# Column sums of the exponentials on TensorE: two tiles each for groups 2 to 7

## The chip, the cores and the metric

The kernel runs on one core of a Trainium2 chip. Five engines work at once, each on its own queue in order: TensorE (PE in the profile, its weight loads PEld), VectorE (DVE), ScalarE (ACT), GpSimd (POOL) and SyncE (SP, which here only starts transfers). The metric is the device time of one execution in microseconds; lower is better.

## The reference

The input is `q`, `k`, `v` for 8 batches, 12 heads, 448 tokens and 64 channels. Cut to what matters:

```
q_n, k_n = rmsnorm(q, g_q), rmsnorm(k, g_k)
scores = q_n @ k_n^T / 8
attn = exp(scores) / sum(exp(scores))       # per query, over the keys
x = attn @ v, heads side by side            # (8, 448, 768)
s = x @ w_gate                              # per token
top 128 tokens of each batch by s:
    out = x + sigmoid(s) * (relu(x @ w1) @ w2)
all other tokens: out = x
```

The change is in the `sum(exp(scores))`, the denominator of the attention, which is a sum over keys for every query.

## The kernel before

All arithmetic is in float32. The work is cut into 24 groups of four heads (three groups a batch, `NG` = 3), and each group into seven units (`NI` = 7) of 64 keys, 168 units in all. Unit `u` is unit `u % 7` of group `u // 7`.

For a unit, `scores` (L290) lets TensorE multiply keys and queries into two score banks out of four (`ps_sc`), and ScalarE takes the exponential of each bank (L299) into a tile `p` of 128 x 2 x 448 numbers. `p` has seven buffers. `values` (L316) multiplies `p` with the values and sums all seven units of a group in two banks `av`; `values_out` copies these away on ScalarE (L343).

Keys lie on the partitions of `p`, so the denominator is a sum over partitions and over the seven tiles of a group. The tiles are first added together on VectorE: `add_probs` (L333) starts with the sum of tiles 0 and 1 in a tile `sum` (two buffers) and adds one more tile at each further unit, a 128 x 896 addition each. `sum_keys` (L362) then sums over the partitions on TensorE: four matmuls with a constant 128 x 32 matrix `pick_pair` write four strips of 32 rows of a bank `den_ps`, 224 columns each. ScalarE copies the bank to `den` (L370), `invert_sums` transposes it on TensorE (L377) and VectorE takes the reciprocals (L379). `to_tokens` transposes the attention output on TensorE (L391), and VectorE multiplies it with the reciprocals into `x` (L393).

For some groups the last tile is not added on VectorE. `add_probs` keeps it in `lasts`, and `sum_keys` puts it through four more matmuls into the same bank, as a second term beside `sum`. Before the change this holds for groups 0 to 5 and for the last one: `sums_last` is `n < 2 * NG or n == n_groups - 1`.

The order of all engines is written out by hand. A loop over `q` issues four units a turn: the scores of two units, the values of the two before them, twice over. Between the pairs stand the pieces of the gated feed-forward part of an earlier batch (`mixture`, L525 to L572) and the `tasks`: `finish` queues, for each group that has ended, `sum_keys`, `invert_sums` and two `to_tokens`. `den_ps`, `denT_ps` and `x_ps` share one bank (`ps_aux`), or one of another pool where no mixture runs, so each of them waits until the one before it has been read.

The other work that the prediction steps on:

- `squares` (L202, ScalarE) and `sum_squares` (L208 on VectorE, L209 and L212 on GpSimd) make the norms of a later group from its tile `tok`; `rows_out` (L226, GpSimd's queue) and `rows_in` (L238, SP's queue) spread them over partitions as `bc`, and `scale_q` (L247, VectorE) scales the queries.
- At the end of a batch `gate` and `spread` (L417 to L438, VectorE) make the gate scores, `score_rows` (L446 on TensorE, L450 on ScalarE) turns them into rows, `count` (L460, VectorE) ranks the tokens with four compare instructions, `annotate` (L475 to L479, VectorE) writes the ranks, and `select` (L487, four indirect transfers on GpSimd's queue) gathers the best 128 tokens in a buffer in memory. `load_selected` (L505) reads them back through SP's queue. That queue works in order and also carries all input tiles (L61), the feed-forward weights (L190) and `bc`.

Of the kernel before, what the change touches and what calls it, by code (L numbers as in the profile page):

```python
# [68 lines left out]
def fast(  # L69
# [27 lines left out]
    NI = S // D  # L97
    H = 2 * NP
    GH = 4
    NG = H // GH  # L100
# [7 lines left out]
    n_groups = B * NG  # L108
# [18 lines left out]
    def aux(shape, name):  # L127

        if PER * now[0] >= units:
            return ps_sc.tile(shape, F32, tag="sc", name=name)  # L130
        if spare[0]:
            return ps_moe.tile(shape, F32, tag="moe", name=name)
        return ps_aux.tile(shape, F32, tag="aux", name=name)
# [144 lines left out]
    probs, sums, avs, xTs, rdens, xs = {}, {}, {}, {}, {}, {}  # L278
# [44 lines left out]

    def add_probs(u):
        n, i = divmod(u, NI)
        if i == NI - 1 and sums_last(n):
            lasts[n] = probs.pop(u)
            probs.pop(u - 1)
            return
        if i > 0:  # L330
            if i == 1:
                sums[n] = p_pool.tile([128, 2, S], F32, name="sum", bufs=2)
            nc.vector.tensor_tensor(  # L333
                out=sums[n], in0=probs[u - 1] if i == 1 else sums[n], in1=probs[u], op=OP.add
            )
            probs.pop(u - 1)
        if i == NI - 1:
            probs.pop(u)

    def values_out(n):  # L340
# [5 lines left out]

    dens, lasts = {}, {}

    def sums_last(n):


        return n < 2 * NG or n == n_groups - 1

    def sum_keys(n):

        ps = aux([128, 512], "den_ps")
        terms = [sums.pop(n)] + ([lasts.pop(n)] if n in lasts else [])
        for t in terms:
            for hh in range(2):
                for odd in range(2):  # L360
                    o = 64 * odd + 32 * hh
                    nc.tensor.matmul(  # L362
                        out=ps[o : o + 32, 0 : S // 2],
                        lhsT=pick_pair,
                        rhs=t[:, hh].rearrange("k (jj odd p) -> k odd jj p", odd=2, p=CP)[:, odd],
                        start=(t is terms[0]),
                        stop=(t is terms[-1]),
                    )
        den = norm_pool.tile([128, NJ // 2, CP], F32, name="den", bufs=1)
        nc.scalar.copy(out=den.rearrange("d j p -> d (j p)"), in_=ps[:, 0 : S // 2])  # L370
        dens[n] = den
# [268 lines left out]
    def finish(n, q):  # L640

        if n == n_groups - 1:
            for fn, args in ((sum_keys, (n,)), (invert_sums, (n,)), (to_tokens, (n, 0))):
                task((q, 1), fn, *args)
            task((q, 1), last_tokens, n)
            return
        task((q, 1), sum_keys, n)
        task((q, 2), invert_sums, n)
        task((q + 1, 0), to_tokens, n, 0)
        task((q + 1, 1), last_tokens, n)  # L650
# [35 lines left out]
    def run_values(upto, q):  # L686
        ended = False
        while waiting and waiting[0] <= upto:
            u = waiting[0]
            if ended and u % NI == 0:  # L690

                return
            values(waiting.pop(0))
            if u % NI == NI - 1:
                values_out(u // NI)
                finish(u // NI, q)
                ended = True
            add_probs(u)
# [580 lines left out]
```

## Time and profile before

| what | value |
|---|---|
| median of 4 runs | 534.6 us (534.34 to 536.62) |
| the profiled execution, its own time | 534.5 us |
| its span, first to last instruction | 532.8 us |
| what lies around the span | 1.7 us |
| mean granted TensorE clock | 0.993 of full speed |

An execution that is profiled gives for every instruction its engine, its line in the code, its start and its duration. A group of equal instructions is written with its count ("x8"), a TensorE group by pipelined matmuls whose durations overlap, so that the distance from one group's start to the next one's, not the duration, is what a group costs. A float32 matmul of the code shows as two records: four matmuls on a `p` tile are "x8". "[0.47 <-ACT den L370]" says that the engine sat idle for 0.47 us before the group and which instruction let it go on.

Busy share of three engines, the clock and the transfers in the stretch where groups 2 to 7 end, from the table of windows (the share of the 16 DMA engines can come out a little over 1):

| stretch, us | length | PE busy | DVE busy | ACT busy | DMA share |
|---|---|---|---|---|---|
| 52 to 64 | 12 | 10.58 | 10.46 | 9.55 | 0.69 |
| 64 to 78 | 14 | 13.35 | 13.55 | 10.89 | 0.63 |
| 78 to 86 | 8 | 7.74 | 7.38 | 5.49 | 1.02 |
| 86 to 94 | 8 | 7.53 | 7.54 | 6.64 | 1.05 |
| 94 to 103 | 9 | 8.65 | 6.91 | 6.08 | 0.81 |
| 103 to 111 | 8 | 7.44 | 5.98 | 6.09 | 1.03 |
| 111 to 126 | 15 | 14.32 | 14.20 | 10.92 | 1.01 |
| 126 to 140 | 14 | 14.00 | 11.95 | 8.29 | 1.06 |
| 140 to 150 | 10 | 10.00 | 5.47 | 4.75 | 0.88 |

The column sums of groups 2 to 7 start on TensorE at 59.00, 76.39, 92.47, 101.86, 118.20 and 142.45 us.

### The profile page before, as it was taken

How to read it: one execution, taken by the hardware profiler on the slowest of the kernel's cores; microseconds unless marked ns; L12 is line 12 of the kernel's file. 1: busy time of each engine (PE TensorE's matmuls, PEld its weight loads, DVE VectorE, ACT ScalarE, POOL GpSimd, SP SyncE). 2: the span in 40 equal slices, each digit the busy share in tenths (PEclk: the TensorE clock that was granted, in tenths of full speed). 3: DMA queues.
4: the chain of work that ended last, by engine and by line, in shares of the span. 5: the costliest groups of instructions: out<-in, count | busy, mean ns of one | idle time of the engine just before them, and what ended most of it. 6: DMA issues, size and time to landing. Idle time of an engine off the chain costs nothing. (4 is left out here: it accounts for less than half of the span.)

```text
span 532.8 us, 16470 instructions
## 1 busy us (share of the span) xinstructions
PE 505.9 (95%) x7116; PEld 285.2 (54%) x7116; DVE 339.7 (64%) x644; ACT 277.9 (52%) x506; POOL 240.6 (45%) x193
## 2 busy tenths in 40 slices
PE   6999899899999999999999999999999999999991
PEld 5444344346644466546644466543665457568770
DVE  2777899789675776659657795668766385443000
ACT  3687787684635755546545755547554354311000
POOL 4784997756724276244734456336742103002000
PEclk9999999999999999999999999999999999999997
DMA  8957859899971497608736486604945032004100
GB/s 300 357 167 250 269 197 345 293 348 292 337 218 36 131 266 219 207 31 222 247 113 209 124 265 208 222 4 126 294 126 139 32 106 62 1 30 134 61 4 33
DMA packets 41605, 93.57 MB, mean 176 GB/s; under 512 B 6454, under 2 KB 24374, under 8 KB 41524
## 3 DMA queue, kind: packets, MB, share of 16 engines
q1 hardware_dynamic: 36772, 85.96, 50.9%
q0 software_dynamic: 4608, 6.47, 3.7%
q8 instruction: 58, 0.95, 0.7%
q14 instruction: 23, 0.19, 0.1%
q10 hardware_dynamic: 144, 0.00, 0.0%
HBM read 74.93 MB, written 25.35 MB: 188 GB/s over the span
## 5 line engine op out<-in xcount | busy, mean ns | idle before, releaser
L299 ACT ACTIVATE p<-sc,rinv 128x448 f32<-128x448 f32 x336 | 186.3, 641 | 101.7 <-PE sc L290 89.4
L290 PE MATMUL sc<-qT,kT 64*32 64x448 f32 x2688 | 151.6, 540 | 0.9 <-ACT p L299 0.6
L316 PE MATMUL av<-p,v 64*32 64x448 f32 x2688 | 146.6, 537 | 0.0
L212 POOL TENSOR_TENSOR rinv<-ss,neg_half 128x14 f32<-128x14 f32 x48 | 137.8, 2872 | 4.0
L333 DVE TENSOR_TENSOR sum<-sum,p 128x896 f32<-128x896 f32 x113 | 122.5, 1084 | 8.9 <-ACT p L299 1.8
L316 PEld LDWEIGHTS av<-p,v 64*32 64x32 f32 x2688 | 54.9, 107 | 71.9 <-issue 65.6
L209 POOL TENSOR_SCALAR ss<-ss 128x14 f32<-128x14 f32 x48 | 22.1, 461 | 155.1 <-DVE ss L208 129.0
L290 PEld LDWEIGHTS sc<-qT,kT 64*32 64x32 f32 x2688 | 48.8, 106 | 71.4 <-issue 47.9
L544 PE MATMUL moe_ps<-xeT,w 128*128 128x128 f32 x576 | 69.2, 277 | 0.0
L544 PEld LDWEIGHTS moe_ps<-xeT,w 128*128 128x128 f32 x576 | 66.2, 192 | 4.3 <-issue 4.3
L393 DVE TENSOR_TENSOR x<-x_ps,rden 112x512 f32<-112x512 f32 x48 | 32.9, 689 | 51.3 <-PE x_ps L391 51.1
L208 DVE TENSOR_REDUCE ss<-sq 128x14 f32<-128x896 f32 x48 | 51.3, 1076 | 22.4 <-ACT sq L202 19.3
L563 PE MATMUL moe_ps<-w,hT 128*128 128x384 f32 x176 | 61.2, 491 | 0.0
L487 POOL DMA_INDIRECT selected<-x,rank x32 | 36.1, 1127 | 35.0 <-DVE x L479 26.2
L202 ACT ACTIVATE sq<-tok 128x896 f32<-128x896 f32 x48 | 46.0, 964 | 8.9 <-DMA tok<-in_tok_dram 8.6
L581 POOL DMA_INDIRECT out_dram<-xe,row x8 | 10.8, 1346 | 77.6 <-DVE rden L379 45.6
L563 PEld LDWEIGHTS moe_ps<-w,hT 128*128 128x128 f32 x176 | 31.7, 190 | 21.8 <-issue 2.9
L417 DVE SCALAR_TENSOR_TENSOR prod<-x,wg 112x256 f32<-112x256 f32 x96 | 40.9, 426 | 3.0
L226 POOL DMA_DIRECT2D rows<-rinv x44 | 29.1, 662 | 6.5 <-POOL rinv L212 6.5
L391 PEld LDWEIGHTS x_ps<-ident,xT 128*112 128x112 f32 x192 | 21.0, 134 | 18.9 <-issue 11.9
L391 PE MATMUL x_ps<-ident,xT 128*112 128x128 f32 x192 | 29.1, 278 | 1.4 <-DVE x L393 1.4
L572 DVE SCALAR_TENSOR_TENSOR xe<-sc,xe 128x384 f32<-128x384 f32 x5 | 3.1, 618 | 41.0 <-PE sc L563 41.0
(66 smaller groups left out, 341.2 us busy)
## 6 DMA issues: line engine op xcount, KB each, us to landing
tok<-in_tok_dram SPq DMA_DIRECT2D x48, 448.0 KB, 6.7
qT<-in_qT_dram SPq DMA_DIRECT2D x24, 448.0 KB, 4.9
kT<-in_kT_dram SPq DMA_DIRECT2D x24, 448.0 KB, 9.1
v<-in_vp_dram SPq DMA_DIRECT2D x24, 448.0 KB, 7.2
out_dram<-x SPq DMA_DIRECT2D x8, 1344.0 KB
bc<-rows SPq DMA_DIRECT2D x44, 224.0 KB, 5.7
xe<-selected SPq DMA_DIRECT2D x8, 385.0 KB, 3.0
w<-in_moe_w_dram SPq DMA_DIRECT2D x6, 512.0 KB
```

What stands on the lines that cost most here:

```text
L202: nc.scalar.activation(out=sq, in_=t, func=AF.Square, scale=scale)
L208: nc.vector.tensor_reduce(out=ss, in_=sq, axis=AX.X, op=OP.add)
L212: nc.gpsimd.tensor_tensor(out=rinv.rearrange(flat), in0=ss.rearrange(flat), in1=neg_half.to_broadcast([128, 2 * NI]), op=OP.pow,)
L290: nc.tensor.matmul(out=scs[hh][o : o + 32, 0:S], lhsT=get("kT", n)[r, c, D * i + k0 : D * i + k0 + 32], rhs=get("qT", n)[r, c, :], start=True,
L299: nc.scalar.activation(out=p[:, hh], in_=scs[hh][:, 0:S], func=AF.Exp, scale=rinvs[n, 1][:, hh, i : i + 1],)
L316: nc.tensor.matmul(out=avs[n][c][o : o + 32, 0:S], lhsT=get("v", n)[r, hh, i, d0 : d0 + 32], rhs=probs[u][r, hh], start=(i == 0), stop=(i ...
L333: nc.vector.tensor_tensor(out=sums[n], in0=probs[u - 1] if i == 1 else sums[n], in1=probs[u], op=OP.add)
L391: nc.tensor.transpose(out=ps[:CP, j, :], in_=t[:, j, :], identity=ident)
L417: nc.vector.scalar_tensor_tensor(out=prod, in0=xs[b][:, j, cols], scalar=1.0, in1=wg[:, cols], op0=OP.mult, op1=OP.mult, accum_out=gates[b ...
L487: w = nc.gpsimd.indirect_dma_start(out=t[:, :], out_offset=bass.IndirectOffsetOnAxis(ap=rank[:, j : j + 1], axis=0), in_=x[:, j, :], in_of ...
L544: nc.tensor.matmul(out=ps[:, 128 * i : 128 * i + n], lhsT=w1[:, dc, 128 * (f0 + i) : 128 * (f0 + i + 1)], rhs=xeT[:, dc, :n], start=(dc == 0),
L563: nc.tensor.matmul(out=ps[:n, : DM // 2], lhsT=hT[:, fc, :n], rhs=w2[:, fc, cols], start=(fc == 0), stop=(fc == NFC - 1),)
```

## The change

`sums_last`, a yes or no for each group, becomes `held`, a count: one tile for groups 0, 1 and 23, two for groups 2 to 7, none for the others. `add_probs` no longer adds a held tile on VectorE, and `sum_keys` puts each held tile through its own four matmuls. `lasts[n]` is a list. Tiles 0 and 1 are let go together at unit 1 and each later one at its own unit, which is bookkeeping in the program that builds the kernel.

```diff
     def add_probs(u):
         n, i = divmod(u, NI)
-        if i == NI - 1 and sums_last(n):
-            lasts[n] = probs.pop(u)
-            probs.pop(u - 1)
+        if i >= NI - held(n):
+            lasts.setdefault(n, []).append(probs.pop(u))
             return
         if i > 0:
             if i == 1:
                 sums[n] = p_pool.tile([128, 2, S], F32, name="sum", bufs=2)
             nc.vector.tensor_tensor(
                 out=sums[n], in0=probs[u - 1] if i == 1 else sums[n], in1=probs[u], op=OP.add
             )
-            probs.pop(u - 1)
-        if i == NI - 1:
+            if i == 1:
+                probs.pop(u - 1)
             probs.pop(u)
...
-    def sums_last(n):
-        return n < 2 * NG or n == n_groups - 1
+    def held(n):
+        return 1 if n < 2 or n == n_groups - 1 else 2 if n < 8 else 0
...
-        terms = [sums.pop(n)] + ([lasts.pop(n)] if n in lasts else [])
+        terms = [sums.pop(n)] + lasts.pop(n, [])
```

Instruction by instruction this leaves ScalarE's, GpSimd's and SP's queues as they were. TensorE gets four more matmuls in the column sums of groups 2, 3, 4 and 5 and eight more in those of groups 6 and 7, 32 in all, each time right behind the matmuls that are there. VectorE loses one addition for each of groups 2 to 5 and two for each of groups 6 and 7, eight in all. Nothing else changes its place.

## The prediction

> **What bounds the kernel now.** I read the page first, then the table of windows around the changed groups, then the timelines of TensorE, ScalarE, VectorE and SP there, then the landings of the transfers.
>
> ```profile
> span 532.8 us, 16470 instructions
> PE 505.9 (95%) x7116; PEld 285.2 (54%) x7116; DVE 339.7 (64%) x644; ACT 277.9 (52%) x506; POOL 240.6 (45%) x193
> ...
> L333 DVE TENSOR_TENSOR sum<-sum,p 128x896 f32<-128x896 f32 x113 | 122.5, 1084 | 8.9 <-ACT p L299 1.8
> ```
>
> TensorE is busy for 95% of the span. The change takes 8 additions of 1.084 us (8.7 us) off an engine with 64% and gives 32 matmuls to the full one. So each added matmul counts unless TensorE would have stood idle, and an addition saved counts only where TensorE, in the end, waits for VectorE. I go through the six places.
>
> **What one held tile costs on TensorE.** With one held tile (group 5) the column sums take from 101.86 to the next group of instructions at 102.76, 0.90 us; with none (group 7) from 142.45 to 142.97, 0.52 us. The difference, 0.38 us, is the price of four matmuls of this form; the distance from the first term's start to the second's (92.47 to 92.87) gives 0.40. Eight such tiles are 8 x 0.38 = 3.0 us if none is hidden. Four matmuls are eight records of 0.35 us, so they overlap: they run in four column strips.
>
> [...]
>
> **Groups 2 and 3: hidden behind ScalarE.**
>
> ```profile
> 61.39 0.43 PE L377 MATMUL denT_ps<-ident,den 128*112 128x128 f32 x2 [1.42 <-DVE prod L417]
> ...
> 78.27 0.43 PE L377 MATMUL denT_ps<-ident,den 128*112 128x128 f32 x2 [0.91 <-ACT den L370]
> ```
>
> ```profile
> 60.95 0.38 ACT L370 COPY den<-den_ps 128x224 f32<-128x224 f32 x1
> ...
> 77.88 0.34 ACT L370 COPY den<-den_ps 128x224 f32<-128x224 f32 x1
> ```
>
> TensorE stands still before the transposition of the sums, because ScalarE has to copy them first. In group 2 the matmuls end at 59.97, but ScalarE reaches the copy at 60.95, behind a square of another group, with no idle time; its end at 61.33 is what releases TensorE (the releaser that the line names, one of VectorE's products, is only the nearest event). With 0.40 more the sums end at 60.37: no cost. In group 3 they end at 77.35, the copy starts at 77.88, again behind a square; group 4 shows that ScalarE starts 0.07 after the last matmul. 77.35 + 0.40 + 0.07 = 77.82: just in time, no cost. Without that cover each would cost 0.38.
>
> **Groups 4 and 5: paid, then swallowed.**
>
> ```profile
> 92.87 0.56 PE L362 MATMUL den_ps<-p,pick_pair 128*32 128x224 f32 x8
> 93.90 0.43 PE L377 MATMUL denT_ps<-ident,den 128*112 128x128 f32 x2 [0.47 <-ACT den L370]
> ...
> 102.27 0.56 PE L362 MATMUL den_ps<-p,pick_pair 128*32 128x224 f32 x8
> 102.76 1.73 PE L290 MATMUL sc<-qT,kT 64*32 64x448 f32 x32
> 104.28 1.71 PE L316 MATMUL av<-p,v 64*32 64x448 f32 x32
> 106.56 2.18 PE L290 MATMUL sc<-qT,kT 64*32 64x448 f32 x25 [0.56 <-ACT p L299]
> ...
> 110.55 0.43 PE L377 MATMUL denT_ps<-ident,den 128*112 128x128 f32 x2
> ```
>
> ```profile
> 104.78 0.95 ACT L202 ACTIVATE sq<-tok 128x896 f32<-128x896 f32 x1 [3.18 <-DMA tok<-in_tok_dram]
> 105.64 0.33 ACT L370 COPY den<-den_ps 128x224 f32<-128x224 f32 x1
> 105.87 4.55 ACT L299 ACTIVATE p<-sc,rinv 128x448 f32<-128x448 f32 x8
> ```
>
> In group 4 ScalarE waits for the sums (its copy starts at 93.50 after 0.35 idle), so TensorE falls back by 0.40; in group 5 by another 0.38, 0.78 at 102.76. But here TensorE is ahead of ScalarE. Two scores and two values take 1.52 + 1.51 + 1.51 + 1.64 = 6.18 us where nothing waits (elsewhere in this timeline), and 102.76 to 110.55 is 7.79: 1.61 lost. ScalarE stands 3.18 us before a square whose tile lands at 104.7, and the exponentials queue behind it without a gap until 110.4; the scores of the next pair need their banks. That landing belongs to SP's queue: the tile is issued at 99.00 behind `xe` (97.17), which waits for the last of the four gathers (landed 97.15), which GpSimd issues after work that starts at 81.51 with a sum of squares of VectorE. None of it hangs on TensorE after 81. Being 0.78 late fits in 1.61, so the stretch ends with ScalarE and this 0.78 costs nothing. The other end: if the landing moves with TensorE, 0.78 is paid in full.
>
> **The saving on VectorE.** VectorE works almost without a gap from 64.98 to 86.63 (20.58 busy of 21.65). Only one removed addition, group 3's at 74.28, lies ahead of a chain that someone waits for: the queries' scaling (its `bc` landed by 74.96, so it can start a microsecond earlier), then the four compares from 77.35, then the sum of squares above. The compares need ScalarE's rows, which end at 77.03, so this moves up by 0.27 at most, and through gathers, SP and tile to ScalarE at 104.78. The stretch is full of transfers (DMA share 1.02 to 1.05 from 78 to 94), where an earlier issue need not land as much earlier. Bounds 0 and -0.27; I take the middle, -0.15. The other seven additions end in front of waits that are not VectorE's own lateness: before the output scaling at 59.11, 101.12 and 117.46 it idles for TensorE already (1.16, 1.36, 0.33), group 4's scaling at 86.63 has nothing waiting behind it before 92.47, and at 136.92 it waits for ScalarE.
>
> **Groups 6 and 7: two tiles each, paid.**
>
> ```profile
> 118.20 0.58 PE L362 MATMUL den_ps<-sum,pick_pair 128*32 128x224 f32 x8 [0.46 <-DVE x L393]
> 119.01 0.55 PE L525 MATMUL moe_ps<-ident,xe 128*128 128x128 f32 x3 [0.22 <-ACT xeT L530]
> 119.39 0.38 PE L377 MATMUL denT_ps<-ident,den 128*112 128x128 f32 x2
> ```
>
> ```profile
> 142.45 0.58 PE L362 MATMUL den_ps<-sum,pick_pair 128*32 128x224 f32 x8
> 142.97 2.94 PE L544 MATMUL moe_ps<-xeT,w 128*128 128x128 f32 x24
> ```
>
> Group 6: the 0.46 before the sums is the bank's turn (VectorE reads the output of the instruction before) and stays. Behind them stands a wait of 0.22 that the new matmuls fill. Then the transposition needs the copy: in group 4 it starts 93.90 - 92.47 = 1.43 after the sums' start with one held tile, with two 1.43 + 0.40 = 1.83, so at 120.03 in place of 119.39: +0.64. Bounds: +0.54 (0.76 less 0.22, if the copy is quicker) and +0.76. Group 7: nothing waits on TensorE from 126 to 150, and 2.8 us of feed-forward matmuls hide the copy: 2 x 0.38 = +0.76, with bounds 0.76 and 0.80.
>
> A held tile also keeps its buffer until the column sums. `p` has seven; tiles 5 and 6 of a group are wanted again by the scores seven units later, and at the sums at most three units beyond the group are scored, so nothing waits for them. Behind 150 the few waits of TensorE (0.29 to 1.22 us) are its own round trips over ScalarE and VectorE and move with it, as does the tail.
>
> **The sum.** 0 + 0 + 0.78 - 0.78 - 0.15 + 0.64 + 0.76 = +1.25 on the profiled execution's 534.5 us (span 532.8 and 1.7 around it), 535.75; the median is 0.1 above that execution, so 535.8.
>
> **Rivals.**
>
> Slower: the wait for the tile at 104.78 swallows nothing. If transfers that TensorE frees late (queries, keys and values wait for its reads in SP's queue) push the tile back by as much as TensorE is late, the 0.78 stays: 0.78 + 0.64 + 0.76 = +2.2, 536.8. It decides once the landing is more than 0.5 later. For it: the DMA engines are full there. Against it: everything in the queue ahead of the tile is issued before 99.00, and only group 4's delay (0.40) precedes that. If group 3's cover, 0.06 wide, fails as well, 537.2; all eight paid is 537.6.
>
> Faster: the relief of VectorE is worth more, because gathers and tile land out of the crowd of weights that are issued from 86.64 on. TensorE can win back no more than the 1.61, of which 0.78 is spent: -0.83. With groups 6 and 7 paid that is +0.57, 535.2; to fall under 534.6 their 1.40 must be hidden too, at the lowest 533.8. For it: VectorE has no gap from 65 to 87. Against it: the compares wait for ScalarE's rows, and 126 to 150 has no idle time to hide in.
>
> Without effect, the additions having been the same work: excluded by the counts, 64 more records on a full engine.
>
> **How the numbers follow.** The forecast has 0.55, with its own range 535.1 (chain full early, bounds low) to 536.4; the slower rival 0.33, the faster one 0.12. What this kernel's measurement can tell from no change is about 0.3%, 1.6 us. The forecast lies within it but for 0.06 that comes out above 536.2; all of the slower rival lies above; of the faster one 0.08 is put beyond the bound for something that the trace doesn't show, 0.04 within. Faster 0.08, same 0.53, slower 0.39. The range 534.7 to 537.1 leaves out the faster rival's low part and the slower one's upper end.
>
> **What would show it.** Records of the sums over held tiles 120 in place of 56, additions 105 in place of 113, VectorE's busy time near 331 us. Groups 2 and 3: transposition still at 61.4 and 78.3. Group 4: 94.3. Then the wait of TensorE near 106.6 shrunk and 110.55 reached at 110.3 to 110.6; a start near 111.3 there would be the slower rival. Group 6's transposition 0.64 later against its own scores, group 7's 0.76. A wait of ScalarE for TensorE before an exponential that stood for VectorE before, or a later landing of the tile, would make it wrong.

## The result, and the profile after

The changed kernel takes 535.99 us (median of 51 runs, 534.71 to 538.88) against 534.71 us for the kernel before (78 runs beside them). The ratio is 1.0024 with a 95% interval of 1.0017 to 1.0031: slower by 1.28 us, between 0.9 and 1.7. The profiled execution took 535.38 us, with a granted TensorE clock of 0.994. Medians and ratios in this document leave out two runs that took far longer than all others of their kernels, one of 663.88 us of the kernel before and one of 1052.79 us in the experiments.

The page of the changed kernel, span, busy times and the group of the additions (every line number behind the edit is one lower than before):

```profile
span 533.7 us, 16584 instructions
PE 508.1 (95%) x7180; PEld 286.7 (54%) x7180; DVE 331.5 (62%) x636; ACT 277.5 (52%) x506; POOL 238.2 (45%) x193
...
L332 DVE TENSOR_TENSOR sum<-sum,p 128x896 f32<-128x896 f32 x105 | 113.8, 1084 | 8.1 <-ACT p L299 1.3
```

64 records more on TensorE, eight additions fewer on VectorE, 331.5 us of VectorE in place of 339.7: the change does what it says.

Before the two traces can be laid side by side, one difference that is not the change's has to go. In the changed kernel's trace everything runs 0.86 us ahead from the first microseconds, because the 36 transposes that open TensorE's work took 5.74 us there and 6.60 us in the trace of before (the last section returns to this). What counts is how this lead of 0.86 shrinks from one group's end to the next. I call the place of an instruction in a trace, less its place in the trace of before, its shift.

Groups 2 and 3, from TensorE's timeline of the changed kernel (start, duration, engine, line, operation, tiles, count, idle time before and releaser):

```profile
60.57 0.43 PE L376 MATMUL denT_ps<-ident,den 128*112 128x128 f32 x2 [1.09 <-ACT den L369]
...
77.45 0.43 PE L376 MATMUL denT_ps<-ident,den 128*112 128x128 f32 x2 [0.53 <-ACT den L369]
```

The idle time before the two transpositions was 1.42 and 0.91 us; 0.33 and 0.38 of it is now work. Shift at both: -0.81. The new matmuls have filled waiting time, and only 0.05 came through.

Groups 4 and 5, the same timeline:

```profile
91.70 0.59 PE L361 MATMUL den_ps<-sum,pick_pair 128*32 128x224 f32 x8
92.11 0.94 PE L361 MATMUL den_ps<-p,pick_pair 128*32 128x224 f32 x16
93.51 0.43 PE L376 MATMUL denT_ps<-ident,den 128*112 128x128 f32 x2 [0.46 <-ACT den L369]
...
102.75 1.73 PE L290 MATMUL sc<-qT,kT 64*32 64x448 f32 x32
104.28 1.71 PE L316 MATMUL av<-p,v 64*32 64x448 f32 x32
105.78 2.15 PE L290 MATMUL sc<-qT,kT 64*32 64x448 f32 x25
...
109.74 0.43 PE L376 MATMUL denT_ps<-ident,den 128*112 128x128 f32 x2
```

Sums to transposition in group 4: 1.81 us, was 1.43. TensorE enters the next stretch at 102.75, as late as before although it started 0.86 ahead: both tiles are paid by then. But 102.75 to 109.74 is 6.99, where it was 7.79; the mark of 0.56 idle before the second scores is gone. The shift at 109.74 is back at -0.81. ScalarE's timeline of the same execution shows where the end comes from:

```profile
103.98 0.95 ACT L202 ACTIVATE sq<-tok 128x896 f32<-128x896 f32 x1 [2.73 <-DMA tok<-in_tok_dram]
104.84 0.33 ACT L369 COPY den<-den_ps 128x224 f32<-128x224 f32 x1
105.06 4.58 ACT L299 ACTIVATE p<-sc,rinv 128x448 f32<-128x448 f32 x8
```

ScalarE again stands before the square whose tile has not landed, and the eight exponentials are queued behind it. From the square's start to TensorE's transposition are 5.76 us here and 5.77 before: the stretch ends by the tile, not by TensorE's arrival.

Groups 6 and 7:

```profile
117.39 0.59 PE L361 MATMUL den_ps<-sum,pick_pair 128*32 128x224 f32 x8 [0.46 <-DVE x L392]
117.80 0.94 PE L361 MATMUL den_ps<-p,pick_pair 128*32 128x224 f32 x16
118.67 0.55 PE L524 MATMUL moe_ps<-ident,xe 128*128 128x128 f32 x3
119.23 0.43 PE L376 MATMUL denT_ps<-ident,den 128*112 128x128 f32 x2
...
142.54 0.58 PE L361 MATMUL den_ps<-sum,pick_pair 128*32 128x224 f32 x8
142.94 0.94 PE L361 MATMUL den_ps<-p,pick_pair 128*32 128x224 f32 x16
143.81 2.94 PE L543 MATMUL moe_ps<-xeT,w 128*128 128x128 f32 x24
```

Group 6 takes 1.84 us from the sums to the transposition, was 1.19: +0.65. Group 7 takes 1.27 from the sums to the projections, was 0.52: +0.75.

Both traces of the changed kernel (the second is run e7 below, on another chip) give this table of the growth of the shift, stretch by stretch:

| from ... to | the prediction's term, us | this trace | e7 |
|---|---|---|---|
| group 0's sums to group 4's sums | 0 | +0.10 | +0.11 |
| group 4's tile | +0.40 | +0.38 | +0.38 |
| group 5's tile and the wait for `tok` | +0.38 - 0.78 - 0.15 | -0.43 | +0.11 |
| group 6's two tiles | +0.64 | +0.65 | +0.64 |
| to the score rows of the batch (L445) | 0 | +0.25 | +0.33 |
| group 7's two tiles | +0.76 | +0.75 | +0.76 |
| from there to TensorE's last instruction | 0 | +0.01 | +0.03 |
| sum | +1.25 | +1.71 | +2.36 |

### The profile page after: what moved, and what is told of

It is laid out like the page before. It is cut to its first block, busy times and chain, and to the rows that moved or that the text cites. A ratio compares the mean times of both kernels' runs of the same rounds, so it can differ in the third digit from the quotient of the medians.

```text
span 533.7 us, 16584 instructions
## 1 busy us (share of the span) xinstructions
PE 508.1 (95%) x7180; PEld 286.7 (54%) x7180; DVE 331.5 (62%) x636; ACT 277.5 (52%) x506; POOL 238.2 (45%) x193
## 5 line engine op out<-in xcount | busy, mean ns | idle before, releaser
L332 DVE TENSOR_TENSOR sum<-sum,p 128x896 f32<-128x896 f32 x105 | 113.8, 1084 | 8.1 <-ACT p L299 1.3
L209 POOL TENSOR_SCALAR ss<-ss 128x14 f32<-128x14 f32 x48 | 20.2, 421 | 158.3 <-DVE ss L208 129.8
L332 DVE TENSOR_TENSOR sum<-p 128x896 f32<-128x896 f32 x24 | 25.7, 1071 | 5.9 <-ACT p L299 5.9
```

The source lines that it names most:

```text
L332: nc.vector.tensor_tensor(out=sums[n], in0=probs[u - 1] if i == 1 else sums[n], in1=probs[u], op=OP.add)
```

## The experiments

The kernels ran in four sessions, each with runs of the kernel before on the same chip: 544.04 us (29 runs) in the first, 542.80 (21) in the second, 534.67 (16) in the third and 535.42 (17) in the fourth. On the first two chips TensorE's instructions came slowly in some stretches without a wait that the profile names, in every kernel that was profiled there, and by its time in the one before too. I call this a shortage of instructions; its cause is not shown (last section). There the totals are blurred, and I read the experiments by their local shifts.

**Only groups 2 to 5, twice (first and second session).**

```diff
-        return 1 if n < 2 or n == n_groups - 1 else 2 if n < 8 else 0
+        return 1 if n < 2 or n == n_groups - 1 else 2 if n < 6 else 0
```

> Two held tiles for groups 2 to 5 only; groups 6 and 7 hold none, as before the change. Theory of the prediction (groups 2 and 3 hidden behind ScalarE's copy, groups 4 and 5 swallowed by the wait of ScalarE for a tile near 104): no change against before, -0.2 to +0.2 us, a ratio of 1.000. Rival A (each of the eight held tiles costs the same share of the measured 1.28 us): +0.64 us, 1.0012. Rival B (all eight tiles are paid at 0.38 us and the saved additions give part of it back): 4 x 0.38 = +1.5 us less whatever group 2 to 5's additions give back, so anything from 0 to +1.5 us, and then the kernel that only saves the additions is faster by as much. In the trace the theory has TensorE's transposition of group 5's sums at the same distance from group 0's column sums as before (74.8 us).

> The same kernel as the first with two held tiles for groups 2 to 5 only, run again because TensorE was short of instructions in several places of those runs. Theory of the prediction: -0.2 to +0.2 us, 1.000. Rival A (equal shares): +0.64 us, 1.0012. Rival B (all paid, additions give back): between 0 and +1.5 us.

Measured: 544.16 us, 1.0001 (0.9984 to 1.0019), and 544.85 us, 1.004 (1.0025 to 1.0055). The same kernel gives two answers on two chips, and their intervals do not overlap, so totals settle nothing on these chips. The reason stands in TensorE's timeline, first of this kernel (e1), then of before:

```profile
88.02 5.27 PE L290 MATMUL sc<-qT,kT 64*32 64x448 f32 x32
```

```profile
88.10 2.08 PE L290 MATMUL sc<-qT,kT 64*32 64x448 f32 x32
```

The same 32 records take 3 us longer, with no wait marked, so TensorE comes to group 4 some 3 us late for a reason that has nothing to do with the tiles. That made this an unplanned test of the swallowing: where TensorE is that late anyway, ScalarE's wait for the tile is over before TensorE needs the exponentials, and the stretch should cost its bare work and nothing be swallowed. It was so: 106.64 to 112.82 in e1 and 106.69 to 112.86 in its repetition, 6.18 and 6.17 us; the prediction had summed 6.18 for the bare work. From group 4's sums to that transposition the shift fell by 0.84 in both, 1.61 won less the price of two tiles.

**Only groups 6 and 7, twice (first and second session).** Groups 0 to 5 and the last hold one tile as before.

```diff
-        return 1 if n < 2 or n == n_groups - 1 else 2 if n < 8 else 0
+        return 1 if n < 6 or n == n_groups - 1 else 2 if n < 8 else 0
```

> One held tile for groups 2 to 5, as before the change, and two for groups 6 and 7. Theory of the prediction: the whole cost is here, 0.64 + 0.76 = +1.4 us, ratio 1.0026; with the 0.25 us that the trace of the changed kernel shows before the score rows of batch 1, +1.65. Rival A (equal shares): +0.64 us, 1.0012. Rival B: 4 x 0.38 = +1.5 us less what two groups' additions give back.

> The same kernel as the one with two held tiles for groups 6 and 7 alone, run again. Theory of the prediction: +1.4 to +1.65 us, 1.0026 to 1.0031. Rival A (equal shares): +0.64 us, 1.0012. If the shortage of instructions shows again, the local distances in the trace tell: group 6's column sums to its transposition 0.64 longer, group 7's 0.76.

Measured: 547.34 us, 1.0057 (1.0038 to 1.0076), and 546.81 us, 1.0068 (1.0047 to 1.0088), more than the tiles can explain, by the same shortage. In both traces the shift grows by 0.65 at group 6 and 0.75 or 0.76 at group 7, as in the changed kernel.

**The additions away without the matmuls, and the matmuls without taking the additions away (first session).**

```diff
-        terms = [sums.pop(n)] + lasts.pop(n, [])
+        terms = [sums.pop(n)] + lasts.pop(n, [])[: 1 if n < 6 or n == n_groups - 1 else 0]
```

> The eight additions are gone from VectorE and the 32 matmuls are not added to TensorE: for groups 2 to 5 the last tile and for groups 6 and 7 the last two are left out of the column sums. It shows what the saving on VectorE is worth by itself. Theory of the prediction: nothing or a little, 0 to -0.27 us, ratio 0.9995 to 1.000. Rival B (all tiles paid, the additions give 1.7 us back): -1.7 us, 0.9968.

```diff
         if i >= NI - held(n):
-            lasts.setdefault(n, []).append(probs.pop(u))
-            return
+            lasts.setdefault(n, []).append(probs[u])
+            if i == NI - 1 and n < 6 or n < 2 or n == n_groups - 1:
+                probs.pop(u)
+                return
```

> The 32 matmuls are added to TensorE and the eight additions stay on VectorE, so that the held tiles that were added before count twice. It shows what the matmuls cost by themselves. Theory of the prediction: the same as the change without its saving, +1.4 us, ratio 1.0026 (groups 2 to 5 hidden and swallowed). Rival B: all paid, 8 x 0.38 = +3.0 us, 1.0057. Here the column sums also wait for the later addition; where that is late on VectorE (groups 4 and 5 have their last tile just before the sums) up to 0.7 us may come on top, which the trace would show as a wait of TensorE for VectorE's addition.

Measured: 545.35 us, 1.0019 (1.0003 to 1.0036), and 545.02 us, 1.0007 (0.9994 to 1.002). A kernel with only less work in it came out slower, which is the size of the blur. Locally they are clearer. Without the additions (VectorE 331.4 us busy) the shift stays the same within 0.03 from group 5's transposition (111.63) to 136.8 us, where the next shortage sets in: the additions of group 6 were worth nothing. Those of group 7 come later and cannot be read here. With matmuls and additions (VectorE 339.7) the shift grows by 0.64 at group 6 and by 0.76 at group 7: the price is the matmuls' alone.

**The square later: before and the changed kernel (second session).** The loop that spreads the preparation of the groups over the units sets the squares of group 9 one slot later, so that ScalarE takes exponentials before it comes to the tile.

```diff
-            first = max(s0 - (20 if n > 5 else 17), 0)
+            first = max(s0 - (19 if n == 9 else 20 if n > 5 else 17), 0)
```

> The kernel before with one thing moved: the two squares of group 9 stand one slot later, behind the exponentials of the next pair on ScalarE, so that the late tile near 104 us no longer holds these exponentials up. No work is changed. Theory of the prediction: the 1.61 us that TensorE loses between group 5's column sums and its transposition go away, -1.6 us at most, -1.0 if the squares hold up the pair after; the distance from the column sums of group 5 to the transposition falls from 8.69 us to 7.1 to 7.7. Rival (the wait is not ScalarE's order): no change, 8.69.

> The changed kernel with the same move of the squares of group 9. Theory of the prediction: what swallowed the matmuls of groups 4 and 5 is gone, so that the change now costs 0.40 + 0.38 more than it did: this run less the one with the square moved in the kernel before is 0.78 + 0.64 + 0.76 = 2.2 us, up to 2.4 with the wait before the score rows. Rival A (each tile costs its share wherever it stands): the difference stays at 1.3 us. In the trace the distance from group 3's transposition to group 5's is longer by 0.78 than in the kernel before with the same move.

Measured: 541.96 us, 0.9982 (0.9962 to 1.0002), and 548.53 us, 1.0097 (1.0075 to 1.0118). TensorE was late already at group 4 (shift +2.65 and +3.25), the wait was no longer there to be removed, and the pair does not test it; the changed kernel with the later square was not run where instructions came in time. The pair gives the price of the two tiles once more: from group 4's sums to group 5's transposition the shift falls by 1.62 with one tile a group and by 0.86 with two; the difference is 0.76.

**The changed kernel again (third session).**

> The changed kernel itself, beside the kernel before on the chip of these runs. If TensorE is not short of instructions here, the theory of the prediction has +1.3 us, 1.0024, as recorded. If it is short of instructions near 88 us as in the runs above, TensorE is already late when it reaches group 4, there is no wait of 1.6 us left to swallow the tiles of groups 4 and 5, and the theory has them paid: 0.76 + 0.64 + 0.76 = +2.2 us, 1.004, with the shortage itself adding a scatter of 1 to 2 us between programs. In the trace, group 6's column sums to its transposition 0.64 longer than before, group 7's to the next feed-forward matmuls 0.76.

Measured: 535.95 us, 1.0023 (1.0012 to 1.0034). In its trace group 5's stretch ended with a shift of +0.59, and the tile was that much later (0.60). ScalarE and then TensorE:

```profile
105.37 0.95 ACT L202 ACTIVATE sq<-tok 128x896 f32<-128x896 f32 x1 [3.26 <-DMA tok<-in_tok_dram]
```

```profile
107.15 2.18 PE L290 MATMUL sc<-qT,kT 64*32 64x448 f32 x25 [0.30 <-ACT p L299]
...
111.14 0.43 PE L376 MATMUL denT_ps<-ident,den 128*112 128x128 f32 x2
```

Square to transposition: 5.77 again. What TensorE's arrival and the tile's each do is best seen in one table of all traces in which the squares stand at their old place. The transposition follows the square where the square is late, and the stretch is the bare 6.17 where it is not (e8 and e9, the next two runs, take longer behind the square; see there):

| kernel | tiles held in 4, 5 | stretch starts | square starts | transposition | stretch | square to transposition |
|---|---|---|---|---|---|---|
| before | 1, 1 | 102.76 | 104.78 | 110.55 | 7.79 | 5.77 |
| after | 2, 2 | 102.75 | 103.98 | 109.74 | 6.99 | 5.76 |
| e7 | 2, 2 | 103.61 | 105.37 | 111.14 | 7.53 | 5.77 |
| e2 | 1, 1 | 105.51 | 107.54 | 113.31 | 7.80 | 5.77 |
| e2b | 1, 1 | 104.47 | 105.09 | 110.89 | 6.42 | 5.80 |
| e1 | 2, 2 | 106.64 | 105.03 | 112.82 | 6.18 | TensorE is last |
| e1b | 2, 2 | 106.69 | 105.07 | 112.86 | 6.17 | TensorE is last |
| e3 | 1, 1 | 105.46 | 104.52 | 111.63 | 6.17 | TensorE is last |
| e4 | 2, 2 | 105.60 | 104.92 | 111.77 | 6.17 | TensorE is last |
| e8 (next) | 1, 1 | 102.95 | 107.26 | 114.26 | 11.31 | 7.00 |
| e9 (next) | 2, 2 | 104.37 | 109.48 | 116.79 | 12.42 | 7.31 |

**The weights earlier: before and the changed kernel (third session).** I thought that the tile lands late because it shares the transfer engines with the feed-forward weights, and issued these earlier.

```diff
-        at(16 + 3 * part, load_w, part)
+        at(10 + 2 * part, load_w, part)
```

> The kernel before with the fourteen loads of the feed-forward weights issued earlier and closer (one every 2 units from unit 10 in place of every 3 from unit 16), so that they are over before the first gathers. Theory: the transfers are no longer full from 78 to 94 us, the tile that ScalarE waits for at 104.78 lands 2 us or more earlier, and TensorE loses none of the 1.61 us: -1.0 to -1.6 us. If the shortage of instructions needs full transfers beside the gathers, its stretch near 88 us goes too, another -1 to -3 us on such a chip; if it needs the gathers alone, it stays. Rival (the tile's landing hangs on the gathers alone): no change. The earlier loads may delay the first groups' tiles between 28 and 60 us by up to 1 us.

> The changed kernel with the weights loaded earlier in the same way. Theory of the prediction: with the wait for the tile gone, the tiles of groups 4 and 5 are paid, so this run less the one with earlier weights in the kernel before is 0.78 + 0.64 + 0.76 = +2.2 us. Rival A (equal shares): +1.3 us.

Measured: 539.50 us, 1.0083 (1.0058 to 1.0109), and 540.85 us, 1.0109 (1.0083 to 1.0134). The difference of 1.35 us, with some 1.4 us of uncertainty on either kernel, does not tell the theory (+2.2) from rival A (+1.3). The idea was wrong: the tile landed later, not earlier. Before with earlier weights, ScalarE, then TensorE, then two rows of the table of windows (stretch, length, busy times with counts of PE, PEld, DVE, ACT and POOL, granted clock, share of the transfer engines, GB/s):

```profile
107.26 0.95 ACT L202 ACTIVATE sq<-tok 128x896 f32<-128x896 f32 x1 [5.46 <-DMA tok<-in_tok_dram]
```

```profile
109.03 3.01 PE L290 MATMUL sc<-qT,kT 64*32 64x448 f32 x25 [2.85 <-ACT p L299]
```

```profile
94.00:103.00 9.00, 8.57 (x162) 3.88 (x166) 7.26 (x9) 6.26 (x12) 8.38 (x7) 1.00 0.98 322
103.00:111.00 8.00, 5.15 (x84) 1.86 (x89) 4.40 (x11) 3.29 (x6) 0.71 (x1) 0.90 1.06 318
```

The transfer engines' share from 94 to 103 rose from 0.81 to 0.98; the tile was issued at 99.61 and landed at 107.18, 7.6 us later, against 99.00 and 104.70 before, 5.7 us. (A landing is the last of the sixteen events that the trace holds for a transfer.) By that share the weights had moved into the crowd, not out of it. The run says something for the theory all the same: with a tile 2.5 us later, TensorE stood 2.85 us where it had stood 0.56, and the transposition came at 114.26 instead of 110.55 (7.00 us after the square where five other traces have 5.76 to 5.80; the granted clock was 0.90 from 103 to 111, but 1.00 there in e9, which took 7.31, so the reason is not shown). In the changed kernel the tile came 4.7 us late (square at 109.48) and the transposition at 116.79; groups 6 and 7 behind it still cost 0.65 and 0.76.

**The square later once more, where instructions came in time (fourth session).** The kernel of e5.

> The kernel before with one thing changed, the squares of group 9 one slot later, on a chip on which the instructions come in time. Theory (ScalarE stands before tile tok with group 5's exponentials queued behind it, and TensorE loses 1.61 us for it; where the squares come later, ScalarE takes the exponentials of that slot first): the stretch of group 5 from 102.75 to the transposition at 110.55 shrinks by 0.8 to 1.6 us and the kernel takes 0.997 to 0.9985 of before, 533.2 to 533.9 us against 534.7. Rival (the late tile is needed a slot later all the same, and what is won is lost before the projections of group 9): the stretch shrinks, but the end does not, ratio 0.9995 to 1.001. Second rival (ScalarE's wait is not what TensorE loses the time for): the stretch stays at 7.8 us. Where TensorE lacks instructions ahead of group 5, all three give no more than 0.998 to 1.002 and the run tells nothing apart.

Measured: 533.70 us against 535.42, 0.9968 (0.995 to 0.9987): faster than the kernel before, and so than the changed one, which was not run beside it. Its trace, TensorE first:

```profile
102.18 1.73 PE L290 MATMUL sc<-qT,kT 64*32 64x448 f32 x32
103.71 1.71 PE L316 MATMUL av<-p,v 64*32 64x448 f32 x32
105.21 1.71 PE L290 MATMUL sc<-qT,kT 64*32 64x448 f32 x32
106.71 1.71 PE L316 MATMUL av<-p,v 64*32 64x448 f32 x32
108.35 0.43 PE L377 MATMUL denT_ps<-ident,den 128*112 128x128 f32 x2
...
117.24 0.58 PE L362 MATMUL den_ps<-sum,pick_pair 128*32 128x224 f32 x8 [1.68 <-DVE x L393]
```

The stretch is 6.17 us, down from 7.79: with ScalarE's wait out of the way TensorE loses none of the 1.62 us. The second rival of this run, that the loss has another cause, is out. But 1.68 us of idle time now stand before group 6's sums, where 0.46 stood, and VectorE's timeline says why:

```profile
113.18 3.40 DVE L333 TENSOR_TENSOR sum<-sum,p 128x896 f32<-128x896 f32 x3
116.50 0.68 DVE L393 TENSOR_TENSOR x<-x_ps,rden 112x512 f32<-112x512 f32 x1
```

VectorE comes to the output scaling straight from three additions; in the trace of before it idled 0.33 us there. It is now the late one. In this trace 1.23 of the 1.62 us are given back: from group 0's sums to TensorE's last instruction the kernel wins 0.38 us, nearer to the rival's amount than to mine, while the runs say 0.7 to 2.7 us. That it is faster is shown, how much of it comes from this stretch is not.

## Why the prediction was right

**Groups 2 and 3, nothing: right.** Their matmuls went into the time in which TensorE waits for ScalarE's copy; in both traces 0.10 or 0.11 us came through up to group 4.

**The price of a tile, 0.38 us: right.** 0.38 at group 4; 0.76 for two at group 7; 0.76 by the difference of e6 and e5. And it is the matmuls' price: it is the same where the additions stay (e4).

**Groups 4 and 5 paid, then swallowed by the wait for `tok`: right, by experiment.** With the tile late, the stretch ended 5.76 to 5.80 us after the square in five traces, of both kinds of kernel, with TensorE's arrival anywhere between 102.75 and 105.51 (7.00 and 7.31 in e8 and e9, where the square starts at 107.26 and 109.48, later still); with TensorE late for another reason the wait was gone and the tiles were paid (6.18 us for the stretch in e1, 6.17 in e4; 0.76 more than e5 in e6); with the wait taken away by order the stretch of the kernel before fell to the bare 6.17 us (e10).

**The slower rival, that the tile moves with TensorE: not borne out, with a remainder.** In one trace of the changed kernel the tile, measured from group 0's sums, landed 0.06 us later than before, in the other 0.60, so that there the sum came to +2.36, about the rival's +2.2. But in e10, where neither VectorE nor TensorE does other work ahead of the tile than before, it landed at 104.75, 0.62 later by the same measure. With the same work ahead of it the landing differed by 0.62 between two executions, so the 0.60 needs no help from the change; that none of it is the change's isn't shown. The traces with the shortage say more: in e1, e1b and e3 to e6 TensorE came to group 4's sums 2.2 to 3.3 us late by this measure, and the tile landed between 0.35 earlier and 0.41 later; in e2 and e2b, with TensorE 2.27 and 2.20 late, it landed 2.30 and 0.82 later. In all eight it was issued between 0.78 earlier and 0.04 later than before: in these traces a late TensorE did not hold it back in SP's queue, which was the rival's mechanism.

**VectorE's saving, -0.15 us: mis-sized, nothing of it arrived.** The prediction took the middle of its bounds of 0 and -0.27. In the changed kernel's traces the first compare moved up by 0.17 us by that measure and GpSimd's last gather by 0.42 and 0.40 (in e10, with no change on VectorE, by 0.00), so the saving did reach the gathers. The issue of the tile moved up by 0.52 and 0.26 (97.61 and 98.73 against 99.00), but the tile took 6.29 and 6.56 us from issue to landing in place of 5.71. Nothing of the earlier issue came out at the landing, in a stretch where the transfer engines' share was 0.87 (97.61 to 103.90 in the changed kernel) and 0.91 (99.00 to 104.70 in before). (In e10 the issue was 0.53 later by this measure, so behind the gathers scatter is as large as the saving.)

**Group 6, +0.64, and group 7, +0.76: right to 0.01 us**, in every trace that holds two tiles there. Reading group 6 off group 4 (copy behind the sums) rather than from 2 x 0.38 less the visible wait (0.54) was the right choice.

**One term was missing: +0.25 to 0.33 us ahead of the batch's score rows.** From the last values' start to L445 TensorE takes 1.85 and 1.92 us in the changed kernel's two traces, 1.64 before. e4 (+0.22) and e9 (+0.28) have it as well; in e2, e2b and e6 the growth there is 0.05, though all three hold the two tiles of group 6. No record names a reason that fits all of them; it stays open.

So the sum of +1.25 met the measured +1.28 with two small errors, of 0.15 and some 0.3, that should have brought it to +1.7, as the pair of traces shows. The mechanism was right place by place; that the sum came within 0.03 of the measurement was luck. Why the medians differ by less than the traces isn't settled. The landing that ends group 5's stretch is one candidate: the one execution of before that was profiled without a shortage had it early, by e10's measure, and so lost less there than others may.

## What to carry to other kernels

Work added to the bound engine was free where that engine was ahead of a transfer that another engine's queue stood on (here 0.78 us within a wait of 1.61); look for the pair "late landing, queue behind it" before counting instructions, and check the cover by the distance from landing to release, which stayed within 5.76 to 5.80 us in five traces while TensorE's arrival moved from 102.75 to 105.51. The same wait is better removed than filled: moving one square behind the exponentials gave the only kernel here that was faster than before (0.9968), until the next engine (here VectorE) became the late one. Relief for an engine off the path is worth what arrives at the end of its chain, and in this stretch, with the transfer engines' share at 0.87 to 0.91, that was nothing that could be told from scatter.

## What the runs showed of the hardware

**The start-up took a different time in each execution.** The transposes that open TensorE's work (engine and operation, count, duration in ns least/median/most, first and last start), in before and after:

```profile
L160 PE MATMUL warm_ps<-ident x36: 272/421/445, 5.2 to 11.5; 128*128 128x128 f32 x36
```

```profile
L160 PE MATMUL warm_ps<-ident x36: 272/273/446, 5.2 to 10.6; 128*128 128x128 f32 x36
```

The records start every 0.21 us first and every 0.11 us later, and the step comes after 24 records in before, 16 in after, 17 in e10 and 28 in e5: 3.4 to 6.0 us after the first. Each record more at the slow pace puts off what follows by 0.1 us (0.21 less 0.11), and the eight more in before than in after make up the lead of 0.86 within 0.1. The profile's column of the granted clock shows 1.00 from 5 to 12 us in both, so the pace has to be read from the records. Between the earliest and the latest step lie 2.6 us; what sets its time is not shown.

**On two of the four chips of the experiments TensorE's instructions came slowly in the same stretches.** Windows of e1 and of before:

```profile
88.00:93.00 5.00, 5.00 (x40) 1.29 (x33) 4.34 (x11) 2.35 (x6) 4.23 (x5) 1.00 1.03 353
```

```profile
88.00:93.00 5.00, 5.00 (x100) 2.27 (x95) 4.65 (x12) 4.92 (x10) 4.23 (x5) 1.00 1.03 365
```

40 matmuls in place of 100, at the same granted clock (1.00) and the same transfer share (1.03), with idle times of 0.57 to 0.61 us before weight loads for which the profile names nothing. It came again near 140, 208, 263, 392 and 452 us in most of these traces, each time where GpSimd issues gathers, and cost 8 to 9 us in all, an estimate from the times of the kernel before in the first two sessions (544.04 and 542.80) against the third (534.67). Full transfer engines are no condition of it: in e1 their share was 0.22 from 452 to 455, where the shift grew by some 1.8 us. The traces of the third and fourth session have the same gathers and no such stretch. No run here shows the cause.
